# A planner of engine order, changed to work in passes and with a queue model of the DMAs

## The chip, the cores and the metric

One NeuronCore of one Trainium2 chip runs the whole kernel. Its engines are TensorE (PE, with its weight loads shown as PEld), VectorE (DVE), ScalarE (ACT), GpSimd (POOL) and SyncE (SP, which only issues DMAs here). Each works through its own queue strictly in order; semaphores make an instruction wait for others. The metric is device time in microseconds of one execution, as the median of several.

## The reference

Attention with normalized q and k, followed by an MLP with a hard-swish:

```python
batch, n_heads, seq, head_dim = (8, 12, 448, 64)
q_n, k_n = (rmsnorm(q, g_q), rmsnorm(k, g_k))      # x / sqrt(mean(x*x) + 1e-6) * g
scores = np.matmul(q_n, k_n.transpose(0, 1, 3, 2)) / np.sqrt(64)
attn = np.exp(scores - max)
attn = attn / (np.sum(attn, axis=-1, keepdims=True) + 1e-09)
x = np.matmul(attn, v)         # heads side by side: 3584 tokens x 768
h = x @ w_in                   # 768 -> 2048
g = h * np.clip(h + 3.0, 0.0, 6.0) / 6.0
out = g @ w_out                # 2048 -> 768, float32
```

## The kernel before

The work is cut into 48 pairs of heads, six for each of the eight batches, and the MLP into one block for each batch. Nothing is issued while the kernel's body runs. Each piece of work is recorded as a `Step` (`Plan.add`, L47): the engine or engines that may do it with an estimated duration, a due time, a function that issues it, the steps that it depends on, and for a DMA the time of its transfer (`xfer`). Buffers come from rings (`Ring.take`, L137), which hand over the former users of a buffer as further dependencies. At the end `Plan.order` (L68) goes forward through time once: it finds the engine that can start something first, and among the steps ready there takes the one with the smallest due time. The list that comes out is issued as it is (L641 to 643), so the order on each engine is fixed before the run, and the hardware waits where the estimate was wrong.

For each pair P these steps are recorded:

- `loads` (L295): k and q into `qk` (five buffers) and v into `vf` (five), by SP; the q of pairs 0 to 2 by ACT. At most eight DMAs of SP and ACT are under way: the ninth waits for the first to land.
- `prep` (L310): squares `sq` (L320 on ACT for pairs 0 to 2, then L322 in halves on DVE or POOL, from batch 2 on L329 on POOL), their sums `ssq` (L337, DVE), the reciprocal root `rs` (L343 and L344, ACT), the scaled `qks` (L351, halves, DVE or POOL) and the cast of v, `va` (L359, POOL).
- `turn`: q and k transposed. For the first ten pairs by PE (L377), with copies to `kp` and `kq` by DVE (L381, L383); later by a DMA transpose (L388), with `kp` by DVE or POOL (L392).
- `attend` (L402): scores by PE (L416, two row tiles of 64 at a time), exponentials by ACT (L421), four to a pair.
- `gather` (L429): attention times v by PE (L437), with the sum as 65th column; DVE divides (L462 and L463; the last 64 rows of three pairs together in L502 and L503), and the result is transposed into `xT`, in batch 0 by PE and DVE (L476, L480), later by a DMA transpose (L486, L511).

The MLP of a batch has 16 groups of h (L533 on PE; L539 on ACT and L541 on DVE make `gT` of it) and six or eight groups of y (L558 on PE, L566 on DVE, stores L585 on SP). Two PSUM buffers `M` serve these groups and the early transposes. The h and y of one batch are spread over the attention of the next by due times made by hand (`begin`, `merge`). The weights come by eight DMAs of POOL (L277, L283).

A step with `lock=True` on DVE or POOL waits in the plan until the other engine's locked step is over (`port`): these are the squares, qks, va and kp of the DMA path. The plan's price of a DMA was one number: SP's and ACT's share one server, POOL's another, and while POOL's transfers run SP's go at 0.425 of their speed (`hard`, L53). A landing is 1.7 us after the transfer, for transposes 1.5 more (`late`).

Of the kernel before, what the change touches and what calls it, by code (L numbers as in the profile page):

```python
# [30 lines left out]
        self.eng = self.start = self.end = None  # L31


class Plan:

    LAT = {"PE": 0.20, "ACT": 0.18, "DVE": 0.15, "POOL": 0.20, "SP": 0.0}
    DMA_LATENCY = 1.7  # L40
    SOFT, HARD = 0.64, 0.425
    AHEAD, HURRY = 0.0, 6.0

    def __init__(self):
        self.steps = []

    def add(self, on, dur, due, fn, *deps, xfer=0.0, after=0.0, lock=False, late=0.0):  # L47
        on, f = ({on: dur}, lambda e: fn()) if isinstance(on, str) else (on, fn)
        s = Step(on, due, f, deps, xfer, after, lock, late, len(self.steps))
        self.steps.append(s)  # L50
        return s

    def hard(self, soft, at, todo):  # L53

        for t0, t1 in soft:
            if t1 <= at:
                continue
            part = min(todo, max(0.0, t0 - at))
            at, todo = at + part, todo - part
            if todo <= 0:  # L60
                return at
            part = min(todo, (t1 - at) * self.HARD)
            at, todo = at + part / self.HARD, todo - part
            if todo <= 0:
                return at
        return at + todo

    def order(self):  # L68
        users = {id(s): [] for s in self.steps}
        left = {}  # L70
        for s in self.steps:
            left[id(s)] = len(s.deps)
            for d in s.deps:
                users[id(d)].append(s)
        free = dict.fromkeys(self.LAT, 0.0)
        port = dma_free = dma_soft = 0.0
        soft = []
        open_ = {e: [] for e in self.LAT}
        ready = {}

        def release(s):
            for e in s.on:
                ready[id(s), e] = max([s.after] + [
                    d.end + (0.06 if d.eng == e and not d.xfer else self.LAT[d.eng]) for d in s.deps])
                open_[e].append(s)

        for s in self.steps:
            if not left[id(s)]:
                release(s)
        done = []  # L90
        while len(done) < len(self.steps):
            best = None
            for e, l in open_.items():
                for s in l:
                    at = max(free[e], ready[id(s), e], port if s.lock and e in ("DVE", "POOL") else 0.0)
                    if best is None or at < best[0]:
                        best = (at, e)
            assert best is not None, "steps wait for each other"
            at, e = best
            near = []  # L100
            for s in open_[e]:
                t = max(at, ready[id(s), e], port if s.lock and e in ("DVE", "POOL") else 0.0)
                if t <= at + self.AHEAD:
                    near.append((s.due + self.HURRY * (t - at), s.n, t, s))
            _, _, at, s = min(near)
            for x in s.on:
                open_[x].remove(s)
            s.eng, s.start = e, at
            free[e] = s.end = at + s.on[e]
            if s.lock and e in ("DVE", "POOL"):  # L110
                port = s.end
            if s.xfer:
                if e == "POOL":
                    at = max(dma_soft, s.end)
                    dma_soft = at + s.xfer / self.SOFT
                    soft.append((at, dma_soft))
                    s.end = dma_soft + self.DMA_LATENCY
                else:
                    dma_free = self.hard(soft, max(dma_free, s.end), s.xfer)
                    s.end = dma_free + self.DMA_LATENCY + s.late  # L120
            done.append(s)
            for u in users[id(s)]:
                left[id(u)] -= 1
                if not left[id(u)]:
                    release(u)
        return sorted(done, key=lambda s: (s.start, s.n))


# [16 lines left out]
def kernel(  # L145
# [17 lines left out]
    PT = S // T  # L163
# [44 lines left out]
    add = plan.add  # L208
# [3 lines left out]
    START, FIRST, PAIR = 9.0, 4.1, 2.3  # L212
    LEAD = 4
    HURRY = 0.8
    WHERE = (0.5, 1.0)

    def h_time(b):
# [77 lines left out]
    def loads(P):  # L295
        at = begin[P]
        qk, war, use = qk_r.take()
        res = []
        cost = 0.62 if P < 3 else 0.85
        for i, src in enumerate((k, q)):  # L300
            e = "ACT" if i and P < 3 else "SP"
            res.append(add(e, 0.47, at - 26, lambda i=i, src=src, e=e: {"ACT": nc.scalar, "SP": nc.sync}[e].dma_start(
                out=qk[0:PT, i], in_=heads(src, P)), *war, xfer=cost, after=max(0.7, at - 24)))
        L[P] = (qk, use, res)
        vf, war, use = vf_r.take()
        s = add("SP", 0.47, at - 19, lambda: nc.sync.dma_start(
            out=vf[0:PT], in_=heads(v, P)), *war, xfer=cost, after=max(0.7, at - 20))
        V[P] = (vf, use, s)

    def prep(P):  # L310
# [54 lines left out]
    def turn(P):  # L365
        at = begin[P]
        qks, qks_use, sc, va, va_use, vc = SC.pop(P)
        kq, war, kq_use = kq_r.take()
        kp, kwar, kp_use = kp_r.take()
        if P < NPE:  # L370
            m, mwar, m_use = M_r.take()
            pt = m[:].bitcast(BF16)[:, 0:2 * S].rearrange("p (i c) -> p i c", i=2)
            tr = []
            for i in range(2):
                def trans(i=i):
                    for t in range(T):
                        nc.tensor.transpose(  # L377
                            out=pt[:, i, t * PT:(t + 1) * PT],
                            in_=qks[0:PT, i, t].rearrange("p h d -> p (h d)"), identity=ident[0:PT, 0:PT])
                tr.append(add("PE", 0.4, at - 2, trans, sc[i], id_make, *mwar))  # L380
            ks = add("DVE", 0.45, at - 1, lambda: nc.vector.tensor_scalar_mul(  # L381
                kp[:, 0:S], pt[:, 0], gp[:, 0:1]), tr[0], g_make, one_make, *kwar)
            qc = add("DVE", 0.45, at - 1, lambda: nc.vector.tensor_copy(out=kq[:, 1], in_=pt[:, 1]), tr[1], *war)  # L383
            m_use += [ks, qc]
            qks_use += tr
            KQ[P] = (kq, kp, va, kq_use, kp_use, va_use, [ks, qc], vc)
        else:
            tr = add("SP", 1.3, at - 8, lambda: nc.sync.dma_start_transpose(  # L388
                out=kq[:].rearrange("p i (t c) -> p (i t) c", c=PT),
                in_=qks[0:PT].rearrange("p i t h d -> p (i t h d)")), *sc, *war, xfer=1.3, late=1.5)  # L390
            ks = add({"DVE": 0.34, "POOL": 0.6}, 0, at - 1, lambda e: (
                nc.vector if e == "DVE" else nc.gpsimd).tensor_scalar_mul(  # L392
                    kp[:, 0:S], kq[:, 0], gp[:, 0:1]), tr, g_make, one_make, *kwar, lock=True)
            qks_use.append(tr)
            kq_use.append(ks)
            KQ[P] = (kq, kp, va, kq_use, kp_use, va_use, [ks], vc)
# [32 lines left out]
    def gather(P):  # L429
# [20 lines left out]
        i = P % 3  # L450
# [34 lines left out]
        else:  # L485
            tr = add("SP", 1.2, at + 0.6 * step, lambda: nc.sync.dma_start_transpose(  # L486
                out=xT[b % 2][:, j, 0:SM].rearrange("p (s c) -> p s c", s=NS),
                in_=xn[:].rearrange("p s a d -> p (s a d)")), xe, *xT_war(b), xfer=0.7, late=1.5)
            xn_use.append(tr)
            G.append(tr)  # L490

        if i == 2:
# [17 lines left out]
            if b % 2:  # L510
                tr = add("SP", 1.2, at + 0.7 * step, lambda: nc.sync.dma_start_transpose(  # L511
                    out=xT[1][:, j - 2:j + 1, SM:SM + 128],
                    in_=xr[:, j - 2:j + 1, :].rearrange("p s c -> p (s c)")), *R["of"], *xT_war(b), xfer=0.7, late=1.5)
                xr_use.append(tr)
                G.append(tr)

# [5 lines left out]
    def xT_war(b):  # L522
        return H_last.get(b - 2, [])
# [26 lines left out]
    def y_group(b, i, n, due, span):  # L550
# [32 lines left out]
                segs.append((ov[b - 1 + e, T - 1, PT - 64:PT, cs], e * 64, e * 64 + 64))  # L583
        for dst, r0, r1 in segs:
            s = add("SP", 0.47, due + span + 3, lambda dst=dst, r0=r0, r1=r1: nc.sync.dma_start(  # L585
                out=dst, in_=y[r0:r1, cs]), *([c] if last else Y_now[b, i, "c"]), xfer=0.5)
            y_use.append(s)

    def mlp(groups, t0, t1):
# [22 lines left out]

    blocks = []

    def weights(c, at, load, kept):
        kept[c] = add("POOL", 0.9, at, lambda: load(c), gate, xfer=4.4, after=at)

    def first():
        nonlocal gate
# [4 lines left out]
    gate = None  # L624
    blocks.append((-0.1, first))
    for c in range(4):
        blocks.append((0.0, lambda c=c: weights(c, W_IN_AT + W_STEP * c, load_w_in, W_in)))
        blocks.append((0.0, lambda c=c: weights(c, W_OUT_AT + W_STEP * c, load_w_out, W_out)))
    for P in range(NP):
        for fn, at in ((loads, -26), (prep, -13), (turn, -2), (attend, 0)):  # L630
            blocks.append((begin[P] + at, lambda fn=fn, P=P: fn(P)))
# [42 lines left out]
```

## Time and profile before

| | us |
|---|---|
| median of 8 runs | 442.68 (440.85 to 443.12) |
| profiled execution | 442.61 |
| its span | 440.7 |
| PE busy | 411.5 (93% of the span) |
| DVE, ACT, POOL busy | 245.4, 249.0, 241.0 |
| first PE instruction | 11.55 |
| first matmul of the MLP (L533) | 45.57 |

The profile shows one execution. Busy time is the union of an engine's instructions; matmuls are pipelined, and their records overlap. Idle time is put down to what ended it. A row with a mean over many instructions hides that the first 60 us and the rest are different stages, so the profile is read by stretches of time. In the chain of work that ended last PE holds 82% of the span and DVE 6%.

The notable durations are, for one instruction: an exponential 0.914 us; a ssq 1.215; a qks half 1.06 on POOL and 0.69 to 0.93 on DVE; a half of squares 1.08 on POOL and 0.68 to 1.29 on DVE; a va cast 0.66; a kp on POOL 1.405. From issue to landing the loads take 3.4 to 4.0, the transposes into kq 3.2 and into xT 2.3.

### The profile page before, as it was taken

The page shows a single profiled execution, that of the slowest core. Times are in us where ns is not written, and L with a number is a line of the kernel's source. Part 1 is how long each engine was busy: PE and PEld are TensorE (multiplying, and loading weights), DVE is VectorE, ACT ScalarE, POOL GpSimd, SP SyncE. Part 2 cuts the span into 40 slices and gives each one's busy share as a digit, 9 for nine tenths or more (in the row PEclk, how much of TensorE's full clock was granted, in tenths as well). Part 3 has the DMA queues.
Part 4 walks back from the last instruction along what each step waited for, and adds up shares of the span by engine and source line. Part 5 has one row for each costly group of instructions (what it writes and reads, how often), then busy time and mean ns, then how long its engine had stood idle before and what let it go on. Part 6 is the DMA issues. An engine that isn't in the chain of part 4 may idle for free.

```text
span 440.7 us, 9205 instructions
## 1 busy us (share of the span) xinstructions
PE 411.5 (93%) x3663; PEld 229.3 (52%) x3682; DVE 245.4 (56%) x417; ACT 249.0 (56%) x425; POOL 241.0 (55%) x230
## 2 busy tenths in 40 slices
PE   0687889999999998999999999999999999999996
PEld 0355445555455565554455555554455555654563
DVE  1998777657664564456565465456564444334421
ACT  3788478557775676457673667457673665123200
POOL 3499898764856657665775666846767510000000
PEclk9999899999999999999999999999999999999999
DMA  8999999978354746584466655684466320220122
GB/s 242 251 267 267 211 223 191 193 180 214 100 143 133 183 120 143 148 210 131 108 163 173 159 138 158 157 211 121 106 162 175 92 59 12 56 80 0 37 71 73
DMA packets 102923, 64.58 MB, mean 147 GB/s; under 512 B 59744, under 2 KB 99424, under 8 KB 102880
## 3 DMA queue, kind: packets, MB, share of 16 engines
q1 hardware_dynamic: 94544, 57.01, 51.1%
q0 software_dynamic: 7296, 6.29, 9.0%
q10 hardware_dynamic: 1040, 0.69, 0.5%
q8 instruction: 29, 0.48, 0.5%
q14 instruction: 14, 0.11, 0.1%
HBM read 45.61 MB, written 11.01 MB: 128 GB/s over the span
## 4 chain that ended last, share of the span: by engine, by line
PE 82%; DVE 6%; DMA 3%; ACT 3%; POOL 3%; issue 2%; SPq 1%; POOLq 0%; DVEq 0%
PE M L558 27%; PE M L533 26%; PE S L416 8%; PE X L437 8%; PE S L558 4%; PE S L533 2%; PE R L437 2%; ACT e L421 2%; DVE ssq L337 2%; DMA qk<-in_k_dram 1%; DVE qks L351 1%; PE X L558 1%; POOL qks L351 1%; DVE sq L322 1%; DMA vf<-in_v_dram 1%
## 5 line engine op out<-in xcount | busy, mean ns | idle before, releaser
L421 ACT ACTIVATE e<-S 112x896 bf16<-112x896 f32 x192 | 166.2, 914 | 64.5 <-PE S L416 64.5
L533 PE MATMUL M<-xT,w_in_sb 128*128 128x384 bf16 (+1 forms) x679 | 146.3, 351 | 4.8 <-DVE gT L541 4.0
L351 POOL TENSOR_TENSOR qks<-qk,rs 112x512 bf16<-112x512 f32 x87 | 91.1, 1062 | 87.9 <-ACT rs L344 87.8
L558 PE MATMUL M<-w_out_sb,gT 128*128 128x384 bf16 x736 | 131.8, 326 | 0.0
L558 PEld LDWEIGHTS <-gT 128*128 128x128 bf16 x896 | 82.9, 98 | 57.9 <-issue 7.8
L533 PEld LDWEIGHTS <-w_in_sb 128*128 128x128 bf16 x768 | 69.9, 98 | 69.6 <-issue 15.0
L541 DVE SCALAR_TENSOR_TENSOR gT<-t,M 128x384 bf16<-128x384 f32 (+1 forms) x116 | 70.8, 612 | 59.8 <-ACT t L539 59.0
L539 ACT ACTIVATE t<-M 128x384 f32<-128x384 f32 (+1 forms) x116 | 62.7, 540 | 68.8 <-PE M L533 65.4
L437 PEld LDWEIGHTS <-e 112*128 112x128 bf16 x1536 | 65.0, 99 | 31.4 <-issue 16.0
L337 DVE TENSOR_REDUCE ssq<-sq 112x16 f32<-112x1024 f32 (+1 forms) x49 | 58.4, 1193 | 25.1 <-POOL sq L329 12.9
L329 POOL TENSOR_TENSOR sq<-qk 112x1024 f32<-112x1024 f32 x36 | 68.2, 1894 | 0.3 <-DMA qk<-in_q_dram 0.3
L416 PE MATMUL S<-kq,kp 64*128 64x448 bf16 x384 | 56.8, 365 | 4.2 <-DVE kp L381 1.7
L437 PE MATMUL X<-va,e 112*128 112x65 bf16 x1152 | 58.5, 195 | 0.8 <-ACT e L421 0.6
L566 DVE COPY y<-M 128x384 f32<-128x384 f32 x46 | 25.6, 556 | 59.3 <-PE M L558 59.2
L359 POOL CAST va<-vf 112x512 bf16<-112x512 f32 x48 | 31.6, 660 | 10.6 <-DMA vf<-in_v_dram 10.3
L392 POOL TENSOR_SCALAR kp<-kq,gp 128x448 bf16<-128x448 bf16 x23 | 32.3, 1405 | 5.0 <-DMA kq<-qks 5.0
L463 DVE TENSOR_TENSOR xn<-X,rd 128x384 bf16<-128x384 f32 x48 | 26.8, 557 | 1.6
L416 PEld LDWEIGHTS <-kp 64*128 64x128 bf16 x384 | 12.3, 94 | 27.7 <-issue 18.1
L437 PE MATMUL R<-va,e 112*128 112x65 bf16 x384 | 20.4, 195 | 0.0
L377 PE MATMUL M<-ident,qks 112*128 112x112 bf16 x80 | 7.8, 238 | 13.0 <-DVE qks L351 12.5
L558 PE MATMUL S<-w_out_sb,gT 128*128 128x384 bf16 x112 | 19.5, 326 | 0.0
L462 DVE RECIPROCAL rd<-X 128x6 f32<-128x6 f32 x48 | 9.2, 192 | 14.9 <-PE X L437 14.7
(42 smaller groups left out, 154.8 us busy)
## 6 DMA issues: line engine op xcount, KB each, us to landing
qk<-in_k_dram SPq DMA_DIRECT2D x48, 224.0 KB, 3.4
vf<-in_v_dram SPq DMA_DIRECT2D x48, 224.0 KB, 4.0
qk<-in_q_dram SPq DMA_DIRECT2D x45, 224.0 KB, 3.6
w_in_sb<-in_moe_w_in_dram POOLq DMA_DIRECT2D x4, 768.0 KB, 11.3
w_out_sb<-in_moe_w_out_dram POOLq DMA_DIRECT2D x4, 768.0 KB, 9.4
out_dram<-y SPq DMA_DIRECT2D x8, 336.0 KB, 3.3
out_dram<-y SPq DMA_DIRECT2D x8, 288.0 KB, 3.3
out_dram<-y SPq DMA_DIRECT2D x8, 240.0 KB, 3.2
```

Of the source, the lines that this page charges most:

```text
L329: parts = [add("POOL", 1.93, at - 10, lambda: nc.gpsimd.tensor_tensor(out=sq[0:PT], in0=qk[0:PT], in1=qk[0:PT], op=MULT), *ld, *war, lock= ...
L337: red = add("DVE", 0.6 * n, at - 8 * hurry + 0.5 * i0, lambda i0=i0, i1=i1, cs=cs: nc.vector.tensor_reduce(out=ssq[0:PT, cs], in_=sq[0:PT, ...
L351: sc.append(add(on, 0, at - 6 * hurry, lambda e, i=i, rs4=rs4: engines[e].tensor_tensor(out=qks[0:PT, i].rearrange("p t h d -> p h t d"), ...
L359: vc = add({"POOL": 0.61}, 0, at - 3, lambda e: engines[e].tensor_copy(out=va[0:PT, :, :, 0:D], in_=vf[0:PT].rearrange("p h (t d) -> p h t ...
L392: nc.vector if e == "DVE" else nc.gpsimd).tensor_scalar_mul(
L416: nc.tensor.matmul(out=ps[:, a, 0:S], lhsT=kp[rows, c0:c0 + 128], rhs=kq[rows, 1, :], start=True, stop=True)
L421: x = add("ACT", 0.93, at + step * (t0 + i) / T + 0.2, lambda t=t0 + i, ps=ps: nc.scalar.activation(out=e[0:PT, t], in_=ps[0:PT, :, 0:S], ...
L437: nc.tensor.matmul(out=dst[:, a * E1:(a + 1) * E1], lhsT=e[0:PT, t, a, c0:c0 + 128], rhs=va[0:PT, a, t, :], start=(first and a == 0 and t ...
L533: nc.tensor.matmul(out=m[:, 0:n], lhsT=w_in_sb[:, kt, f * 128:(f + 1) * 128], rhs=X[:, kt, :], start=(kt == 0), stop=(kt == NKT - 1))
L539: r = add("ACT", 0.08 + n / 1200, due + span, lambda: nc.scalar.activation(out=t[:, 0:n], in_=m[:, 0:n], func=RELU, bias=0.5, scale=1.0 / ...
L541: g = add("DVE", 0.12 + n / 960, due + span, lambda: nc.vector.scalar_tensor_tensor(out=G[:, f, :], in0=t[:, 0:n], scalar=1.0, in1=m[:, 0: ...
L558: nc.tensor.matmul(out=m[:, 0:HALF], lhsT=G[:, f, i * 128:(i + 1) * 128], rhs=w_out_sb[:, f, cols], start=(f == 0), stop=(f == NFT - 1))
```

## The change

`Plan.order` becomes eight rounds. `forward` is the old walk through time, with another model of the DMAs. `backward` then walks the result from its end: on each engine it packs the steps as late as their users allow, in reverse order of their starts, and writes the start that comes out into `due`, in place of the due time made by hand. The next forward round uses these. Of the eight orders the one whose last step ends first in the plan is issued. The DMA model `Queues` holds one queue each for SP, ACT and POOL; a transfer is a number of descriptors of a size, the heads of the queues take turns, and an SP or ACT DMA starts only when the eighth last one has landed. Each `xfer` is given as (descriptors, bytes), and the 0.15 to 0.20 us of an engine's hand-over is no longer added to a landing. Nothing that is computed, no buffer and no count of instructions changes; DVE takes 8 of the qks halves instead of 9 and 10 of the kp instead of 15, POOL the others. The new line numbers are 90 higher from `loads` on.

```diff
+class Queues:
+    ENTER, DONE = 1.15, 0.3
...
+    def issue(self, s, at):
+        n, size = s.xfer
+        self.rings[s.eng].append([s, float(n), 0.034 + size * 2.34e-5, at + self.ENTER])
+        if s.eng != "POOL":
+            self.issued.append(s)
+
+    def lane(self):
+        return self.issued[-8].end if len(self.issued) >= 8 else 0.0
+
+    def advance(self, until):
+        while True:
+            heads = [r[0] for r in self.rings.values() if r]
...
+            on = [h for h in heads if h[3] <= self.now + 1e-9]
+            turn = sum(h[2] for h in on) * (0.9 if len(on) > 1 else 1.0)
...
 class Plan:
+    PASSES = 8
-    DMA_LATENCY = 1.7
-    SOFT, HARD = 0.64, 0.425
-    AHEAD, HURRY = 0.0, 6.0
...
-    def hard(self, soft, at, todo):
...
     def order(self):
+        best = None
+        for n in range(self.PASSES):
+            got = self.forward()
+            end = max(s.end for s in got)
+            if best is None or end < best[0]:
+                best = (end, [(s, s.eng, s.start, s.end) for s in got])
+            if n < self.PASSES - 1:
+                self.backward(got)
...
+    def backward(self, got):
...
+        def stop(s):
+            t = min(free[s.eng], last[id(s)] - (s.end - s.start - s.on[s.eng]))
+            return min(t, port) if s.lock and s.eng in ("DVE", "POOL") else t
+
+        for _ in got:
+            at, e = max((stop(s), e) for e, l in open_.items() for s in l)
+            s = max((s.start, s.n, s) for s in open_[e] if stop(s) >= at)[2]
+            open_[e].remove(s)
+            s.due = at - s.on[e]
+            free[e] = s.due
+            if s.lock and e in ("DVE", "POOL"):
+                port = s.due
...
+    def forward(self):
...
             for s in open_[e]:
-                t = max(at, ready[id(s), e], port if s.lock and e in ("DVE", "POOL") else 0.0)
-                if t <= at + self.AHEAD:
-                    near.append((s.due + self.HURRY * (t - at), s.n, t, s))
-            _, _, at, s = min(near)
+                t = start(s, e)
+                if t is not None and t <= at:
+                    near.append((s.due, s.n, s))
+            s = min(near)[2]
...
-        cost = 0.62 if P < 3 else 0.85
-                out=qk[0:PT, i], in_=heads(src, P)), *war, xfer=cost, after=max(0.7, at - 24)))
+                out=qk[0:PT, i], in_=heads(src, P)), *war, xfer=(14, 1024), after=max(0.7, at - 24)))
...
-                in_=qks[0:PT].rearrange("p i t h d -> p (i t h d)")), *sc, *war, xfer=1.3, late=1.5)
+                in_=qks[0:PT].rearrange("p i t h d -> p (i t h d)")), *sc, *war, xfer=TURN)
...
-                out=dst, in_=y[r0:r1, cs]), *([c] if last else Y_now[b, i, "c"]), xfer=0.5)
+                out=dst, in_=y[r0:r1, cs]), *([c] if last else Y_now[b, i, "c"]), xfer=(max(1, (r1 - r0) / 16), 1536 if last else 3072))
...
-    def weights(c, at, load, kept):
-        kept[c] = add("POOL", 0.9, at, lambda: load(c), gate, xfer=4.4, after=at)
+    def weights(c, at, load, kept, size):
+        kept[c] = add("POOL", 0.9, at, lambda: load(c), gate, xfer=(48, size), after=at)
```

The values are `TURN, TURN2 = (16, 1400), (16, 700)`; `TURN2` stands for the transposes into `xT`.

## The prediction

> **What bounds the kernel now.** I read the busy time in stretches first, then the waits of TensorE, then the start of the timeline. The profiled execution took 442.61 us, of which the span is 440.7; the 1.9 us around it stay. The median of the eight runs, 442.68, is the same for this purpose. Each row below gives length, then busy time with the number of instructions for PE, PEld, DVE, ACT and POOL.
>
> ```profile
> 0.00:12.00 12.00, 0.45 (x4) 0.32 (x4) 2.48 (x5) 4.46 (x10) 3.37 (x18) 1.00 0.91 241
> 12.00:20.00 8.00, 4.36 (x29) 1.75 (x28) 8.00 (x10) 5.09 (x11) 4.51 (x5) 1.00 1.14 257
> 20.00:30.00 10.00, 9.20 (x127) 6.11 (x124) 9.50 (x18) 8.31 (x13) 8.60 (x9) 1.00 1.16 272
> 30.00:40.00 10.00, 8.77 (x128) 5.48 (x127) 8.90 (x20) 8.91 (x14) 9.55 (x11) 1.00 1.17 256
> 40.00:46.00 6.00, 3.79 (x48) 2.00 (x49) 5.64 (x11) 3.89 (x7) 6.00 (x6) 0.89 1.19 260
> 46.00:62.00 16.00, 13.38 (x140) 7.95 (x138) 11.62 (x21) 9.19 (x22) 13.88 (x16) 0.94 1.23 224
> 62.00:345.00 283.00, 280.29 (x2547) 154.21 (x2560) 163.58 (x275) 179.08 (x304) 190.26 (x166) 1.00 0.64 157
> 345.00:436.00 91.00, 90.90 (x659) 51.45 (x660) 35.16 (x64) 30.04 (x49) 4.84 (x4) 1.00 0.19 50
> 436.00:440.70 4.70, 0.36 (x3) 0.00 (x0) 0.56 (x1) 0.00 (x0) 0.00 (x0) 0.99 0.29 64
> ```
>
> There are two regimes. From 62 us on PE is busy 280.29 + 90.90 of 374 us, so only 2.8 us of idle time are left there, and no other engine passes 68%. Before about 46 us DVE is the full engine (32.0 of the 34 us from 12 to 46), POOL and ACT lie close behind, and PE works in short bursts. In the timeline the first matmul of the MLP (L533) stands at 45.57. So the question is when that matmul can start, and whether PE stays fed afterwards. All that PE waited for directly is short:
>
> ```profile
> PE M L377 <- DVE qks L351: 12.5, 3, 11.6
> PE M L533 <- DVE gT L541: 4.0, 4, 1.6
> PE M L476 <- DVE xn L463: 2.0, 2, 1.5
> PE S L416 <- DVE kp L381: 1.7, 1, 1.7
> ```
>
> Of the first, 11.6 us are the start itself: loads, squares and rstd of pair 0.
>
> [...]
>
> ```profile
> 15.46 0.90 POOL L277 DMA_DIRECT2D w_in_sb<-in_moe_w_in_dram  x1
> 15.99 2.56 DVE L322 TENSOR_TENSOR sq<-qk 112x512 f32<-112x512 f32 x1
> 16.36 0.63 POOL L359 CAST va<-vf 112x512 bf16<-112x512 f32 x1
> 16.94 1.05 POOL L322 TENSOR_TENSOR sq<-qk 112x512 f32<-112x512 f32 x1
> 19.26 0.56 PE L416 MATMUL S<-kq,kp 64*128 64x448 bf16 x2 [1.67 <-DVE kp L381]
> 41.55 2.14 DVE L351 TENSOR_TENSOR qks<-qk,rs 112x512 bf16<-112x512 f32 x2 [0.19 <-ACT rs L344]
> ```
>
> The same DVE square takes 0.68 us [...] (at 34.89 us, and POOL's cast beside it then 1.13 instead of 0.63), here 2.56 behind two POOL operations. [...]issued starts of L533 with 384 columns follow each other by 0.162 us while one record lasts 0.33. Hence I use the idle time only as a ceiling of what can be won. [...] No DMA time is cheaper through the change: it moves the same bytes by the same instructions.
>
> **The change, part by part.** Every instruction stays (96 q and k loads, 48 v loads, 88 transposes by DMA, 192 exponentials, 3682 matmuls); only order and the choice between DVE and POOL move. I compared the two programs' instruction orders and multiplied by the durations of the profile before.
>
> 1. *The start.* The first loads are reordered on SP: k0 k1 k2, q and k of pairs 3 and 4, then v0 to v4; before, v0 and v1 stood among the first five. ACT's queue is the same: q0 q1 q2, the four small g loads, then the squares. Its last g load waits for the fourth transfer of SP's queue in both kernels, and the first square followed it at 8.76 us. Equal size, equal place: 0 us, so the first PE instruction stays at 11.55. If the lanes behave differently, the cost is one transfer, up to 1 us (between the issues on SP at 5.73 and 7.50 lie two of them).
>
> 2. *DVE up to the last transpose copy of batch 0* (L480, sixth; the next thing is the first L533). By prefix sums DVE had 31.7 us of work ahead of it, now 29.4: one ssq more (+1.2), three qks fewer (-2.1), one square fewer (-0.7), one norm of the rest later (-0.8). Before, DVE began at 9.43 and reached that copy at 45.24: 35.8 us for 31.7 of work[...]. With the same 4.1 the first L533 comes 2.3 us earlier, at 43.3.
>
> 3. *The same from ACT's side.* ACT's work up to the 24th exponential is 28.2 + 0.9 us in both orders. It starts at 8.76, so it could end at 37.9; before it ended at 41.17. From there to the first L533 went 4.4 us, of which about 1.3 are the two qks on DVE at 41.55, which stood ahead of the last xn. They are moved behind. So 3.1 us remain, and the first L533 lies between 41.0 (ACT never waits) and 44.3 (it waits as before).
>
> 4. *What stands against it.* In the new order DVE has two locked operations, a square and a qks, ahead of kq and kp of pair 1, where it had one, and POOL has a chain of squares and qks behind each other there. [...]the scores of pair 1 at 20.9 instead of 19.26. From there twenty exponentials (18.3) and four rstd (1.7) without a gap end at 40.9, and the first L533 is at 44.0: a gain of 1.6. Parts 2 to 4 give gains of 2.3, 1.3 to 4.6 and 1.6; I take 2.4, since the following pairs' kq and kp now come earlier in DVE's queue, so that ACT should be gapless.
>
> 5. *POOL.* Casts va of pairs 0 to 4 now have 7.1, 7.2, 8.3, 7.2 and 5.3 us more of POOL work ahead of them, the sixth only 0.1. POOL was idle at 10 to 20 us (4.51 of 8 from 12 on), so va0 moves from 7.66 to about 20. Its user, the first L437, stood at 19.74, and is itself moved behind more scores. Cost 0[...]; va2 is the tight one: POOL work alone places it at 26.1, and its user stood at 29.33.
>
> 6. *PE.* Ahead of the first L533 stand 26 pairs of score matmuls instead of 28; V blocks and transposes are equal. Two pairs at about 0.36 are done later: +0.7. Afterwards switches away from score matmuls are 104 instead of 105, and the last 92 blocks are in the same order. 0 us.
>
> 7. *Middle.* DVE stays 2.5 to 3.7 us of work ahead, POOL 4 to 8 behind, with kp on POOL 28 times instead of 23 at 1.4 us. POOL waits 87.8 us for rs in all, which hides 7 us. The waits of L533 on gT (4.0) can shrink or grow; I take -0.4. SP's order keeps each kq transpose within a few places. 0, with -2.8 (all idle gone) and +3 (one transpose late on PE by the longest wait of kp on kq, 3.3 us) as ends.
>
> Sum: -2.4 + 0.7 - 0.4 = -2.1, so 440.5 us.
>
> **The rivals.**
> - *Part of it is given back and no difference is left*: POOL does the work that DVE lost at 1.05 instead of 0.69 us[...]; three qks and a square cost 1.4 more there. -2.3 + 1.4 + 0.7 is -0.2, so 442.4. For it: POOL is busy 9.55 of 10 us at 30 to 40. Against: POOL's added work falls into its idle start.
> - *Slower: the lock in the first pairs.* [...]the scores of pair 1 move past 22.5; from there 20.0 of ACT and the 3.1 give 45.6, the old start. That is the point from which it decides. If va2 is also POOL-bound by 1 to 2 us, the first L533 is at about 47.3, and with 0.7: 445.0. For it: POOL's chain there has no gap until it needs rs of pair 3, which itself needs DVE's square. Against: at 21.45 and 41.55 DVE got in between two POOL operations.
> - *More than forecast*: ACT gapless from 15 us and most of the waits of 46 to 62 gone: -4.6 + 0.7 - 2.2, so 436.5. For it: an order with deadlines worked back from the end should feed gT first. Against: DVE's and ACT's orders there are nearly the old ones.
> - That the change does nothing is excluded: DVE's, POOL's and SP's orders differ from their first few steps on.
>
> **How the numbers follow.** Forecast 0.43 (own range 438.5 to 441.7), more 0.10, no difference 0.17, slower 0.30. A difference under 0.2% (0.9 us) cannot be told from none. So faster 0.53, same 0.17, slower 0.30. The range 435.5 to 446.5 takes in the ends of part 7 and both outer cases.
>
> **What would show it.** Right: first L533 at 42 to 44 us, DVE's qks 8 instead of 9, PE idle under 3 us from 62 on, first PE instruction at 11.5. Wrong: scores of pair 1 after 22.5 us, ACT idle on PE's scores in 20 to 40 us, or a PE wait on kp or xT in the middle that was not there.

## The result, and the profile after

The changed kernel takes 451.65 us (median of 11 runs, 448.32 to 453.44) where the kernel before took 442.43 beside it: a ratio of 1.0207, 95% interval 1.0186 to 1.0228. It is 9.2 us slower. The forecast was 440.5, range 435.5 to 446.5. The medians of e4, e7 and e16 below leave out executions that took over 1.5% longer than the quickest of the same kernel.

The profiled execution took 448.32 us, its span is 446.5. It is the quickest of the eleven, so its profile explains 5.7 of the 9.2 us; a slower execution follows in e15. The stretches are cut as in the view of before; the columns are length, then busy time with the number of instructions of PE, PEld, DVE, ACT and POOL, then the granted clock, the share of the DMA engines and GB/s.

```profile
30.00:40.00 10.00, 9.28 (x151) 6.21 (x151) 9.04 (x20) 9.94 (x17) 9.73 (x12) 1.00 1.07 238
...
46.00:62.00 16.00, 13.38 (x107) 7.12 (x106) 13.92 (x18) 9.25 (x18) 12.49 (x15) 0.83 1.26 220
62.00:345.00 283.00, 278.32 (x2524) 152.35 (x2538) 153.56 (x268) 176.27 (x301) 192.57 (x166) 0.99 0.66 155
```

From 46 to 62 us PE is busy for the same 13.38 us as before, but with 107 matmuls instead of 140, at a clock of 0.83 instead of 0.94: equal busy time, less work. The first MLP matmul (L623, before L533) stands at 44.33 us, 1.24 earlier than before. The first y matmul (L648) stands at 81.84, before at 75.96. From there to the end of the span both take about 364.7 us. So in this execution a gain of 1.2 is followed by a loss of 7.1, and all of that loss lies between these two events.

The waits, with total, times and longest, show what TensorE's gaps end with (4.0 us before), and a wait of POOL for a transpose:

```profile
PE M L623 <- DVE gT L631: 5.9, 5, 2.2
...
POOL kp L482 <- DMA kq<-qks: 31.5, 22, 3.7
```

Before, this wait of POOL was:

```profile
POOL kp L392 <- DMA kq<-qks: 5.0, 5, 3.3
```

TensorE's two longest gaps in this stretch end at 57.63 and 78.62 (a third, of 1.04 us, at 67.76). The timeline shows one chain for each (start, length, engine, line, then the idle time before and what ended it). The first:

```profile
51.72 0.94 POOL L374 DMA_DIRECT2D w_out_sb<-in_moe_w_out_dram  x1
...
52.43 2.96 DVE L412 TENSOR_TENSOR sq<-qk 112x512 f32<-112x512 f32 x1
52.68 1.06 POOL L441 TENSOR_TENSOR qks<-qk,rs 112x512 bf16<-112x512 f32 x1
53.67 1.17 POOL L449 CAST va<-vf 112x512 bf16<-112x512 f32 x2
53.78 0.49 ACT L629 ACTIVATE t<-M 128x384 f32<-128x384 f32 x1
...
55.92 1.21 DVE L427 TENSOR_REDUCE ssq<-sq 112x16 f32<-112x1024 f32 x1
...
57.05 0.54 DVE L631 SCALAR_TENSOR_TENSOR gT<-t,M 128x384 bf16<-128x384 f32 x1
...
57.63 1.18 PE L623 MATMUL M<-xT,w_in_sb 128*128 128x384 bf16 x5 [2.12 <-DVE gT L631]
```

The square on DVE takes 2.96 us instead of 0.68 (at 34.89 in the kernel before): it starts beside a DMA issue of POOL, three more POOL instructions (a qks and two casts) follow without a gap, and it ends 0.55 us after the last of them. The gate (`gT`, the multiplication that makes the input of the MLP's second product) had its input at 54.27 and stands behind the square, a qks and a row sum until 57.05. The second:

```profile
71.12 1.41 POOL L482 TENSOR_SCALAR kp<-kq,gp 128x448 bf16<-128x448 bf16 x1 [3.12 <-DMA kq<-qks]
...
73.90 0.49 ACT L629 ACTIVATE t<-M 128x384 f32<-128x384 f32 x1
...
74.51 1.89 POOL L419 TENSOR_TENSOR sq<-qk 112x1024 f32<-112x1024 f32 x1
...
76.43 1.22 DVE L427 TENSOR_REDUCE ssq<-sq 112x16 f32<-112x1024 f32 x1 [2.80 <-POOL sq L419]
...
77.56 1.01 DVE L631 SCALAR_TENSOR_TENSOR gT<-t,M 128x384 bf16<-128x384 f32 x2
...
78.62 1.99 PE L623 MATMUL M<-xT,w_in_sb 128*128 128x384 bf16 x6 [2.25 <-DVE gT L631]
```

Here `kp` stands at the head of POOL's queue and waits 3.12 us for a transpose (issued at 62.06, landed 9.0 us later). A qks pair (2.04) and the squares stand behind it, DVE's row sum waits for the squares, and two gates stand behind the row sum, one with its input there since 74.4.

The transposes themselves landed no sooner in the kernel before: of those into `kq` issued between 44 and 82 us, the median took 5.5 us there and 4.0 here, and the one issued there at 62.27 took 7.5. But there `kp` stands behind a qks pair and the squares and finds its data when its turn comes, at almost the same time:

```profile
67.40 2.04 POOL L351 TENSOR_TENSOR qks<-qk,rs 112x512 bf16<-112x512 f32 x2 [1.30 <-ACT rs L344]
69.40 1.89 POOL L329 TENSOR_TENSOR sq<-qk 112x1024 f32<-112x1024 f32 x1
71.27 1.41 POOL L392 TENSOR_SCALAR kp<-kq,gp 128x448 bf16<-128x448 bf16 x1
```

So what changed here is the place of `kp` in POOL's queue, not the landing.

Each of these two gaps costs more than itself. Two stretches of 3.41 us about the second, columns as above:

```profile
75.34:78.75 3.41, 1.16 (x27) 0.95 (x26) 2.29 (x4) 1.04 (x3) 3.41 (x3) 1.00 0.66 163
78.75:82.16 3.41, 3.41 (x20) 1.52 (x19) 1.92 (x5) 2.07 (x4) 3.41 (x5) 0.50 0.57 170
```

After a stretch in which TensorE is busy for 1.16 of 3.41 us (34%), its clock is 0.50 for the next 3.41 us. About the first gap it is the same (1.29 us or 38% from 54.86, then 0.50). The three half-clock stretches of this execution last 3.41 us each and start at 44.62, 58.27 and 78.75, so 13.65 and 20.48 us apart: 4 and 6 times 3.41. In the 3.41 us ahead of them TensorE was busy for 53, 38 and 34%. In the kernel before it was 55% (41.24 to 44.65), and once 68% (from 30.5 us in e18).

This gives an account of the stretch. From the first h matmul to the first y matmul TensorE has about 26.5 us of work at full clock; the rest is its gaps (the time in which no matmul record runs) and half of the time at half clock. The columns are us:

| profile | first h | first y | between | gaps | at half clock | between - gaps - half of it |
|---|---|---|---|---|---|---|
| before | 45.57 | 75.96 | 30.39 | 2.77 | 2.49 | 26.4 |
| changed | 44.33 | 81.84 | 37.52 | 5.96 | 9.92 | 26.6 |
| changed, again (e15) | 46.42 | 85.18 | 38.76 | 6.96 | 11.38 | 26.1 |
| e10 | 46.45 | 80.50 | 34.06 | 4.51 | 6.83 | 26.1 |
| e13 | 44.37 | 77.40 | 33.03 | 2.90 | 6.82 | 26.7 |
| e18 | 47.59 | 81.58 | 33.99 | 3.73 | 6.76 | 26.9 |

Of the 7.1 us, 3.2 are gaps and 3.7 (half of 9.92 - 2.49) are clock. Where a gap lies inside half-clock time the sum counts part of it twice; so e1 below, with a gap of 7.9 us that does, comes out at 23.5 in the last column.

### The profile page after: what moved, and what is told of

Same layout as the page of the kernel before. It is cut to its first block, busy times and chain, and to the rows that moved or that the text cites. A ratio compares the mean times of both kernels' runs of the same rounds, so it can differ in the third digit from the quotient of the medians.

```text
span 446.5 us, 9209 instructions
## 1 busy us (share of the span) xinstructions
PE 414.9 (93%) x3663; PEld 229.9 (51%) x3682; DVE 237.3 (53%) x411; ACT 247.8 (56%) x425; POOL 246.4 (55%) x236
## 4 chain that ended last, share of the span: by engine, by line
PE 78%; POOL 6%; DVE 5%; DMA 5%; issue 3%; ACT 1%; SPq 1%; ACTq 0%; POOLq 0%
PE M L623 28%; PE M L648 24%; PE S L506 8%; PE X L527 7%; PE S L648 4%; DMA kq<-qks 3%; POOL qks L441 3%; PE R L527 2%; PE S L623 2%; DVE ssq L427 2%; DMA qk<-in_q_dram 1%; POOL sq L412 1%; PE X L648 1%; DVE sq L412 1%; POOL va L449 1%
## 5 line engine op out<-in xcount | busy, mean ns | idle before, releaser
L623 PE MATMUL M<-xT,w_in_sb 128*128 128x384 bf16 (+1 forms) x679 | 150.1, 356 | 8.6 <-DVE gT L631 5.9
L648 PE MATMUL M<-w_out_sb,gT 128*128 128x384 bf16 x736 | 131.3, 326 | 0.0
L648 PEld LDWEIGHTS <-gT 128*128 128x128 bf16 x896 | 83.5, 98 | 57.3 <-issue 6.1
L623 PEld LDWEIGHTS <-w_in_sb 128*128 128x128 bf16 x768 | 70.2, 99 | 75.7 <-issue 22.7
L527 PEld LDWEIGHTS <-e 112*128 112x128 bf16 x1536 | 64.6, 99 | 28.5 <-issue 15.2
L482 POOL TENSOR_SCALAR kp<-kq,gp 128x448 bf16<-128x448 bf16 x28 | 39.3, 1404 | 40.3 <-DMA kq<-qks 31.5
L527 PE MATMUL X<-va,e 112*128 112x65 bf16 x1152 | 55.8, 195 | 0.1
L449 POOL CAST va<-vf 112x512 bf16<-112x512 f32 x48 | 30.1, 630 | 21.5 <-DMA vf<-in_v_dram 11.0
L527 PE MATMUL R<-va,e 112*128 112x65 bf16 x384 | 20.4, 196 | 0.0
L648 PE MATMUL S<-w_out_sb,gT 128*128 128x384 bf16 x112 | 19.5, 326 | 0.0
```

What stands on the lines that cost most here:

```text
L449: vc = add({"POOL": 0.61}, 0, at - 3, lambda e: engines[e].tensor_copy(out=va[0:PT, :, :, 0:D], in_=vf[0:PT].rearrange("p h (t d) -> p h t ...
L527: nc.tensor.matmul(out=dst[:, a * E1:(a + 1) * E1], lhsT=e[0:PT, t, a, c0:c0 + 128], rhs=va[0:PT, a, t, :], start=(first and a == 0 and t ...
L623: nc.tensor.matmul(out=m[:, 0:n], lhsT=w_in_sb[:, kt, f * 128:(f + 1) * 128], rhs=X[:, kt, :], start=(kt == 0), stop=(kt == NKT - 1))
L648: nc.tensor.matmul(out=m[:, 0:HALF], lhsT=G[:, f, i * 128:(i + 1) * 128], rhs=w_out_sb[:, f, cols], start=(f == 0), stop=(f == NFT - 1))
```

## The experiments

### Which part of the change loses

Theory A: the due times worked back from the end put the wrong step first. Theory B: the new price of the transposes, without the old 1.5 us of margin, makes the plan count on landings that come later. e1 keeps the queue model and makes one round, so the hand-written due times decide; e2 is the kernel before with eight rounds on its old price; e3 uses the worked-back due times up to 44 us of the plan and the hand-written ones after; e4 the reverse.

```diff
-    PASSES = 8
+    PASSES = 1                       (e1, from the changed kernel)
+    PASSES = 8                       (e2, in the kernel before, with the rounds and backward)
-                    near.append((s.due, s.n, s))
+                    near.append((s.due if cut is None else s.won if at < cut else s.hand, s.n, s))    (e3; e4 swaps won and hand)
```

> The changed kernel with one forward pass only: the new queue model of the DMAs stays, due times are those made by hand. Theory A (the loss comes from due times worked back from the end: they put gT of the first MLP batch behind DVE steps that wait for POOL[...], so PE runs dry between 44 and 82 us): 441 to 444, first y copy at 76 to 78 us. Theory B (the queue model orders loads and transposes wrongly, and PE waits follow from late data): 449 to 452, as the changed kernel.

> The kernel before with the eight forward and backward rounds, but the old price of the DMAs. Theory A: 447 to 453, with PE waits on gT of 1.5 us and more between 44 and 82 us. Theory B: 440 to 443.

> The changed kernel with the worked-back due times up to 44 us of the plan and the ones made by hand from there. Theory A: the start keeps its gain (first L623 near 44.3) and the loss between 44 and 82 us goes: 440 to 443. Theory B: 448 to 452, since the loads keep their order.

> The mirror of it: due times by hand up to 44 us of the plan, worked back from the end afterwards. Theory A: 448 to 453, the loss stays. Theory B: as the queue model is in both, also 448 to 452; a time below 444 would say that the first 44 us hold the cause.

Measured: e1 457.32 (ratio 1.0342, 1.0306 to 1.0378), e2 446.79 (1.011, 1.0067 to 1.0153), e3 447.09 (1.0105), e4 453.48 (1.0231). None of the four lies in the range that either theory gave. Neither part is harmless, and they do not add up: the queue model alone costs 14.8 us, the rounds alone 4.3, both together 9.2. In the timeline of e1 the model's fault is plain:

```profile
65.15 4.74 SPq L478 DMA_TRANSPOSE kq<-qks  x1
...
71.88 0.34 DVE L482 TENSOR_SCALAR kp<-kq,gp 128x448 bf16<-128x448 bf16 x1 [8.70 <-DMA kq<-qks]
...
72.73 1.12 PE L623 MATMUL M<-xT,w_in_sb 128*128 128x384 bf16 x3 [7.89 <-DVE gT L631]
```

A `kp` waits 8.70 us at the head of DVE's queue for a transpose whose issue alone took 4.74, with gates behind it; from 67.19 the clock is at half for 10.2 us.

e11 asks for the front alone: the worked-back due times for the steps up to 41 us, the order itself placed by the old pass with the old price.

```diff
-        return [x[0] for x in best[1]]
+        return self.forward_old(CUT)      (CUT = 41.0: worked-back due times before it, hand-written ones after; old DMA price)
```

> The kernel before with the changed kernel's worked-back due times for the steps that the queue model places before 41 us of its plan; the order itself is placed by the kernel before's pass, with its price of the transposes, and the due times after that are the hand-written ones. If the gain of the front (first L533 1.2 us earlier) can be had without the loss between 44 and 82 us, the time is 440.5 to 442; if the loss comes from any move of the front (kq and kp of the next heads arriving otherwise), 445 or more.

447.27 (1.0117, 1.0093 to 1.0141). That is the slower outcome. The front's gain cannot be had by itself this way: the first MLP matmul came at 46.87, and gaps of 1.42 and 1.04 us up to 54.1 were followed by half clock.

### The margin of the landings

e5 takes the margin from the kernel before; e6 gives 2.5 us to the changed kernel's three DMA transposes, e7 the same to e1. e8 corrects durations instead.

```diff
-... xfer=1.3, late=1.5)                              (and 0.7 for xT, twice)
+... xfer=1.3, late=0.0)                              (e5, kernel before)
-... xfer=TURN)                                       (and TURN2, twice)
+... xfer=TURN, late=2.5)                             (e6; e7 with PASSES = 1)
-            ks = add({"DVE": 0.34, "POOL": 0.6}, 0, at - 1, lambda e: (
+            ks = add({"DVE": 0.9, "POOL": 1.4}, 0, at - 1, lambda e: (        (e8, with lock=True on the weight loads)
```

> The kernel before, with nothing changed but the 1.5 us by which its plan makes each DMA transpose land late: 0 in its place (three lines). Margin theory (the old price of transposes is too high and so keeps kp and the h groups away from data that may be late; the new price has none of that): slower, 445 to 455, with DVE or POOL waiting at kp for kq while gT stands behind it. Theory that the new queue model hurts by the order of its loads: 441 to 444, as loads stay nearly where they were.

> The changed kernel, with 2.5 us added to the landing of each DMA transpose in the plan (three lines), eight rounds. Margin theory: 441 to 446. Otherwise: 449 to 453.

> The same 2.5 us in the queue model with one forward pass and due times made by hand (457.3 without them). Margin theory: 441 to 447, and the gap of 7.9 us before L623 at 72.7 us is gone. Otherwise: 455 to 459.

> The changed kernel, with measured durations in the plan where they were far off (kp 0.9 on DVE and 1.4 on POOL instead of 0.34 and 0.6[...]; L629 0.10 and L631 0.03 us longer). If the stalls on gT come from too short durations on DVE and POOL: 442 to 447. If they come from late transposes or from the worked-back due times: 449 to 453.

e5 442.59 (1.001, 0.9991 to 1.0028): no difference. The margin is not what carries the kernel before. e6 447.48 (1.0122) and e7 446.69 (1.0101): back by 4.2 of 9.2 and 10.6 of 14.8, so in the new model it matters. e6 is still slower than its expectation of 441 to 446, and the margin moves the whole plan, the choice between DVE and POOL too, so these two don't say which landing it was. e8 456.62 (1.0309) is worse than either of its ranges: with these durations alone corrected, the order has its first MLP matmul at 52.22, and TensorE waits up to 5.5 us for `xn` and 6.5 us for a gate.

### What one gap costs

e10 is the kernel before with dead fills of three y tiles ahead of the tenth gate; nothing else moves.

```diff
+            if s.gate:
+                n += 1
+                if n == GAP_AT:                  (GAP_AT = 10)
+                    for y in y_r.bufs:
+                        nc.vector.memset(y[:], 0.0)
```

> The kernel before with three VectorE fills of y tiles (dead work) put ahead of the tenth gate multiply, so that TensorE meets one gap of 1 to 2.5 us in the first MLP batch and nothing else is moved. It prices a gap. If a gap over about 2 us also brings a stretch of half clock of 3.4 us, the time is 3 to 4 us over the kernel before (445 to 446) and the records show a second half-clock stretch after the fills; if a gap costs only its own length, or is caught up later, 0 to 2 us (442 to 444).

445.88 (1.0076, 1.0048 to 1.0103): 3.4 us for a gap of 1.70. The gap in the timeline, and the window that holds it with the one that follows:

```profile
69.10 0.56 PE L378 MATMUL M<-ident,qks 112*128 112x112 bf16 x8 [1.70 <-DVE gT L542]
```

```profile
67.15:70.56 3.41, 1.71 (x42) 1.48 (x40) 3.30 (x6) 1.48 (x4) 0.29 (x1) 1.00 1.32 136
70.56:73.97 3.41, 3.22 (x16) 1.28 (x13) 2.15 (x6) 1.92 (x4) 3.22 (x3) 0.50 1.38 177
```

The gap and half of 3.41 us at half clock make the 3.4 us. This price is not certain for every such gap: in the profiles of e5 and e9 gaps of 1.98 us (at 76.87) and 1.95 us (at 79.25) were not followed by half clock.

### Is it the gates that stand behind other steps?

e9 moves, in VectorE's order of the first MLP batch alone, each gate ahead of up to three other steps that don't feed it (eight gates); e12 does the same to e6.

```diff
-        return [x[0] for x in best[1]]
+        return self.gates_first([x[0] for x in best[1]], 40.0, 75.0)
```

> The changed kernel with one edit to VectorE's order alone: in the first MLP batch (plan 40 to 75 us) a gate multiply that stands behind up to three other VectorE steps (the squares, the row sums, a reciprocal pair, a qks) is moved ahead of them where nothing of theirs feeds it; SyncE, GpSimd, ScalarE and TensorE keep the changed kernel's order. If the loss is gates that are ready and stand behind a blocked VectorE instruction, the TensorE gaps before the second L623 group near 57.6 and near 78.6 us go, their two half-clock stretches go with them, the first y matmul comes at 76 to 78 us instead of 81.8, and the time is 442 to 446. If the loss is the transposes or a general shift of the front's data (kq, xT late for TensorE itself), the first y matmul stays after 80 and the time at 450 to 453.

> The kernel of e6 (the changed kernel with 2.5 us put on each of the three transposes' landings in the plan) and the edit of e9 together. If late transposes and gates behind blocked VectorE steps are two separate parts of the loss, this is faster than both e6 (447.5) and e9, 442 to 445. If the margin already did what the gates' order does, it stays within 1 us of e6.

e9 450.02 (1.0172, 1.0141 to 1.0202), e12 448.88 (1.0138). The gain hoped for did not come: the gaps moved instead of going. e9 falls on the second side of its expectation by its time and its first y matmul (81.19), though the waits still end with gates; e12 lies 1.4 us above e6, where less or the same was expected. In e9 the square takes 0.69 us again (at 55.29), but ScalarE stands in order too. Its `t`, which feeds the gate, stood behind a `rs` that waited for a row sum which was now later:

```profile
57.74 0.22 ACT L448 ACTIVATE rs<-ssq 112x16 f32<-112x16 f32 x1 [2.96 <-DVE ssq L442]
...
58.91 0.86 ACT L644 ACTIVATE t<-M 128x384 f32<-128x384 f32 x2
...
60.03 1.78 PE L638 MATMUL M<-xT,w_in_sb 128*128 128x384 bf16 x6 [3.02 <-DVE gT L646]
```

At the second chain the edit moved one of the two gates; the other still stands behind the row sum, with a gap of 1.95 us. So moving the last link of the chain is no cure here; e18 below takes away the first.

### The w_out load

The four w_out loads (768 KB each), with the loads of q, k and v beside them, keep the 16 DMA engines full until about 70 us (in the changed kernel the DMA share is 1.27 from 46 to 70 us and 0.74 from 70 to 82). The change moved these loads as well: they are issued at 46.1, 49.2, 51.7 and 59.7 us instead of 39.0, 45.1, 54.3 and 58.8, and the last lands at 70.3 instead of 67.2. No run here moves them alone. e13 and e14 leave out seven eighths of their bytes, in the changed kernel and in the one before, with the orders untouched. e16 and e17 keep the bytes but load four row blocks of full width instead of eight of half width.

```diff
-            out=w_out_sb[:, f0:f0 + NFT // 2, cols],
+            out=w_out_sb[:, f0:f0 + 1, cols],            (e13, e14; the tile is zeroed by VectorE at the start)
+            out=w_out_sb[:, f0:f0 + NFT // 4, :],        (e16, e17; f0 = c * (NFT // 4); in e17 y part p waits for load p)
```

> The changed kernel, its order untouched, but each of the four w_out loads moves one of its eight row blocks (1/8 of the bytes; the rest of the weight tile is filled with zeros by VectorE before the first q arrives, so 7/8 of the load is left out and the MLP's second product isn't the reference's). It takes the load off the 16 DMA engines between 35 and 72 us. If late transposes beside the saturated DMA engines are what starves TensorE between 44 and 82 us, the gaps at 57.6 and 78.6 go with their half-clock windows, the first y matmul comes at 74 to 77 and the time falls to 442 to 445. If the order itself is to blame (steps of one engine in a row that block one another, whatever the DMA does), the first y matmul stays at 80 or later and the time above 448.

> The kernel before with the same 7/8 of the w_out load left out, as the partner of e13. It had 2.8 us of TensorE gaps between its first L533 and its first y matmul, so little can be won: 440 to 442.5. If saturation is the cause of the changed kernel's loss, e13 comes within 2 us of this run; if the order is, e13 stays 6 to 9 us above it.

> The changed kernel, its order untouched, with each w_out load taking four row blocks over all 768 columns instead of eight row blocks over 384: the same bytes in half as many rows, each twice as long. It should shorten the stretch in which the DMA engines are full (until about 70 us in the changed kernel)[...]. If the landings are what starves TensorE, the time falls by 1 to 5 us (446.5 to 450.5); if the bytes alone set the loads' time, it stays within 1 us of 451.6.

> The kernel before with the same wider w_out loads, its order untouched but for them. It had few TensorE gaps in the loaded stretch, so 441 to 443 either way; under 441 would make it quicker than both kernels.

e13 445.53 (1.0059, 1.0036 to 1.0081) is close to the first of its two outcomes, e14 445.59 (1.0073, 1.0048 to 1.0098) outside its own. Without the load the two take the same time, though not for one reason, since e14 has a new gap of its own (below). What counts is that the changed kernel wins 6.1 us. Its transposes into `kq` between 45 and 82 us land after 2.7 us (median) instead of 4.0, the longest after 3.0 instead of 9.0. The second chain is gone, the same `kp` finds its data there:

```profile
67.35 1.41 POOL L482 TENSOR_SCALAR kp<-kq,gp 128x448 bf16<-128x448 bf16 x1
...
72.91 1.21 DVE L427 TENSOR_REDUCE ssq<-sq 112x16 f32<-112x1024 f32 x1
```

The first chain's gap is halved, to 1.09 us at 56.5, where POOL's issue of the smaller load takes 0.60 us instead of 0.94.

The kernel before lost 3.0 us through the same edit, where none was expected, and 3.9 through the wider rows of e17: 446.68 (1.0097, 1.0078 to 1.0116). Both have a gap of 4.1 to 4.2 us at 48 that the kernel before had not. In e17:

```profile
43.05 4.86 DVE L351 TENSOR_TENSOR qks<-qk,rs 112x512 bf16<-112x512 f32 x2 [0.19 <-ACT rs L344]
...
44.48 1.03 POOL L322 TENSOR_TENSOR sq<-qk 112x512 f32<-112x512 f32 x1
45.47 0.81 POOL L283 DMA_DIRECT2D w_out_sb<-in_moe_w_out_dram  x1
```

The same pair of qks took 2.14 us at 41.55 in the kernel before, where both were done at 43.7. Here POOL has a row of four instructions (cast, square, load, square) from 43.9 to 47.3, and the pair ends 0.56 us after it, at 47.9. The order is the same; in e17 only POOL's issue is 0.13 us shorter and the load is shaped otherwise. That the kernel before is quick partly because its DVE operations happen to fall well beside POOL's row is the author's reading of the timelines, not tested by itself.

e16 447.11 (1.0097, 1.006 to 1.0133) is within what was expected, but its executions reach from 443.57 to 449.58 even so, and the profiled one took 452.94, so it says little. No version here is quicker than the kernel before.

### Does the loss belong to the order?

e15 is the changed kernel, profiled once more.

> The changed kernel itself, profiled a second time, since the first profiled execution (448.3) was its quickest. The gaps on gates near 57.6 and 78.6 should be there again if they are the order's own; if they depend on when a transfer happens to land, at least one is gone or another is there. Either way the stretch from the first L623 to the first y matmul should be about 26.5 us plus its TensorE idle time plus half of its half-clock time, and a slower execution should have more of one of the two.

453.16 in one execution. Both gaps are there again with the same chains (the square takes 2.89 us this time). The first MLP matmul came at 46.42, 0.9 us later than in the kernel before, so the front's gain is gone; the first y matmul came at 85.18, and 366.1 us remained. The second gap is longer, as the transpose landed 10.1 us after its issue:

```profile
74.37 1.41 POOL L482 TENSOR_SCALAR kp<-kq,gp 128x448 bf16<-128x448 bf16 x1 [4.38 <-DMA kq<-qks]
...
79.67 1.22 DVE L427 TENSOR_REDUCE ssq<-sq 112x16 f32<-112x1024 f32 x1 [4.06 <-POOL sq L419]
...
81.87 1.44 PE L623 MATMUL M<-xT,w_in_sb 128*128 128x384 bf16 x4 [3.51 <-DVE gT L631]
```

### One swap in GpSimd's order

e18 takes the first link of the second chain away: the one waiting `kp` goes behind the qks pair and the squares that stood behind it. Nothing else moves on any engine, and the load stays.

```diff
 GpSimd's order, changed kernel -> e18
-TensorScalarPtr kp_96<-kq_93,gp 128x448
 TensorTensor qks_88<-qk_70,rs_84 112x2x4x64 x2
 TensorTensor sq_79<-qk_71 112x1024
+TensorScalarPtr kp_96<-kq_93,gp 128x448
```

> The changed kernel with one swap in GpSimd's order and no other: the kp that waited 3.12 us for its kq transpose at 71.1 us goes behind the qks pair and the squares (L419) that stood behind it. If the second chain is kq late, kp waits, the squares behind it late, VectorE waits for them in its row sums, the gate behind those late, TensorE dry, then the gap before the L623 group at 78.6 (2.25) and its half-clock stretch go, together about 4 us: 447 to 448.5, and the gap at 57.6, which has another cause, stays. If the gap is TensorE running ahead of what the engines can deliver there at all, it comes back within 5 us of its old place and the time stays at 450.5 to 453.

446.31 (1.0092, 1.0057 to 1.0128): 5.3 us of the 9.2 come back from the move of one instruction, more than the 4 expected.

```profile
60.88 3.86 PE L634 MATMUL M<-xT,w_in_sb 128*128 128x384 bf16 x12 [2.11 <-DVE gT L642]
...
77.03 4.17 POOL L493 TENSOR_SCALAR kp<-kq,gp 128x448 bf16<-128x448 bf16 x3
77.08 1.22 DVE L438 TENSOR_REDUCE ssq<-sq 112x16 f32<-112x1024 f32 x1 [0.33 <-POOL sq L430]
```

The row sum now waits 0.33 us for the squares instead of 2.80; TensorE has no gap over 0.4 us between 72 and the first y matmul, and its clock is 1.00 from 64.6 us on. The first gap (2.11, now at 60.88) is left as expected. This profiled execution was e18's slowest, 5.9 us longer in span than the profile of before: 2.0 because its first MLP matmul came at 47.59, 3.6 in the middle, where the first gap with its half clock (2.1 + 1.7) is the largest item, and 0.3 after. By the medians e18 still lies 4.4 us above the kernel before.

## Why the prediction was wrong

Its sign was wrong. The term that failed is part 7, the middle.

- *Start (part 1)*: 0 us was right. The first PE instruction came at 12.05, but executions with the order of before began at 12.23 (e10) too.
- *First MLP matmul (parts 2 to 4)*: the gain is not shown. The first profile looks like it: forecast 43.3 to 44.0, measured 44.33, and scores of pair 1 at 20.24 (forecast 20.9). The 4.1 us that part 2 keeps are 35.8 - 31.7; the step from 19.26 to 20.9 in part 4 (1.6 us) was the author's estimate; the profile shows 0.98. But the same order up to there reached it at 46.42 in e15 and 47.59 in e18, and the order of before at 45.57 and, in e10, 46.45. The near hit was luck as far as these few executions tell. Exponentials on ScalarE run almost without a gap from 30 to 40 us (9.94 of 10), as supposed.
- *POOL's casts (part 5)*: right, no wait of L527 on `va` is in the view.
- *PE (part 6)*: forecast +0.7, measured +0.2 in TensorE's work between the two events (26.4 to 26.6); the stretch after the first y matmul is equal.
- *The middle (part 7)* is the step that failed. "The waits of L533 on gT (4.0) can shrink or grow; I take -0.4 ... 0, with -2.8 ... and +3 (one transpose late on PE ...) as ends." The middle measured +7.1 in the first profile (gaps 3.2, clock 3.7) and +8.4 in e15. Two premises were false. First, that POOL's 87.8 us of waits for `rs` hide 7 us of work that moves: a total over the whole kernel was used as cover at one place. Of the 87.8 us, 79.4 lie after 82 us. From 44 to 82 us the profile of before has only

```profile
POOL qks L351 <- ACT rs L344: 4.6, 4, 1.6
```

After 82 us `kp` waits most (28.4 of 31.5 us) and TensorE loses nothing; at 71 us the `kp` in front of the queue made exactly the wait that reached the gates (e18: 5.3 us). Second, the bound of +3 counted a late transpose once, as idle time on PE. The clock, which made 3.4 us of a gap of 1.70 (e10), was not priced, though the profile of before showed a clock of 0.94 from 46 to 62. Of the signs that it named, PE idle under 3 us from 62 on failed: it is 4.7 us from 62 to 345 alone.
- *The slower rival* (two more DVE operations in the first pairs as long as the square at 15.99, 2.56 us) looked at the wrong place: pair 1 was on time, and a square at 52.43 took 2.96 us instead. There it is a gate that is late. `lock` and `port` are rules of the plan; of the hardware the traces show how long these operations took beside POOL's, not why.
- SP's order of the `kq` transposes is beside the point: under the same order of SP the longest landing was 9.0 us beside the w_out load (10.1 in e15) and 3.0 in e13.

Shown: the price of a gap (e10), that the second chain runs through the waiting `kp` (e18), that 6.1 us of the loss go with the w_out bytes (e13), though the same edit costs the kernel before 3.0. Argued from the timeline and not undone by itself: the first chain, the square at 52.43. e9 took the gate from behind it and met another queue. Not tested: whether the w_out loads at their old times would suffice. Open: why the planner's rounds on the old price (e2) and the front alone (e11) each make a gap of their own there.

## What to carry to other kernels

In in-order queues, put a step that waits for a DMA behind ready steps that other engines need (e18), and look first at the stretch in which the DMA engines are full (here a DMA share of 1.27 from 46 to 70 us); a plan that prices landings too early can put such steps in front. Allow for twice the length of a new TensorE gap near 2 us, since half clock may follow (3.4 us for a gap of 1.70 in e10). Cover has to be read at the place of the move, not from a total over the span.

## What the runs showed of the hardware

- Between 24 and 430 us half clock (0.50) came in stretches of 3.41 us, or several in a row (10.2 us in e1); in the changed kernel their starts lie 13.65 and 20.48 us apart, multiples of 3.41. Among all kept traces, windows at full clock in which TensorE was busy up to 68% (e18, from 30.5 us) were followed by it, and windows from 47% on (e9, from 77.4 us; 52% at 54.89 in the kernel before) were followed by full clock. So the busy share of the window alone does not decide it in these records.
- The views show a clock of 1.00 also where there is no record of it yet, up to 24.2 us in the kernel before and 27.6 in the changed one. There a score matmul takes 0.55 us (median), close to the 0.565 of half-clock time (44.7 to 45.1 in the kernel before) and not to the 0.36 at full clock. That TensorE ran at half speed up to there is the author's estimate from these three times.
- Three times DVE's squares or qks took long beside a row of POOL instructions and ended 0.55 to 0.56 us after it: a square 2.96 us (0.68 at 34.89 in the kernel before) beside one DMA issue, one qks and two casts; a pair of qks 4.86 in e17 instead of 2.14; the square at 15.99 in the kernel before 2.56, beside a DMA issue, a cast and a square. The square at 21.45 there took 1.53 and ended 0.9 us before the pair of qks on POOL beside it. Between e17 and the kernel before, where the pair took 2.14, POOL's timing differed by some tenths of a us. These are times of single instructions; their cause was not shown.
- A transpose by DMA from SBUF to SBUF, into `kq`, landed 3.2 us after its issue (median after 82 us, in both kernels), and beside the weight loads after up to 7.5 us in the kernel before, 9.0 and 10.1 in the changed one and 12.3 in e1.
